# Windowed attention and two dense layers on one core: packed scores in 32-query strips, a third packed unit, new order keys and an early sine

## The chip, the cores and the metric

The kernel runs on one core of a Trainium2 chip. The metric is the device time of one execution in microseconds (us). Times come from repeated executions; the profile is of one execution.

## The reference, cut to what matters

Three steps follow one another: attention in which a query sees its own and the 63 keys before it, a dense layer with a squared ReLU, and a dense layer with h·cos(h). All arithmetic is on float32 values.

```python
# q, k, v: (4, 8, 576, 64)
scores = scale * np.matmul(q, k.transpose(0, 1, 3, 2))
rel = pos[:, None] - pos[None, :]
mask = (rel >= 0) & (rel < 64)
scores = np.where(mask, scores, -1e9)
scores = scores - np.max(scores, axis=-1, keepdims=True)
attn = np.exp(scores)
attn = attn / (np.sum(attn, axis=-1, keepdims=True) + 1e-09)
x = np.matmul(attn, v)            # then 2304 tokens x 512
h = np.maximum(x @ w_in, 0.0)     # w_in: 512 x 2048
x = h * h @ w_out                 # w_out: 2048 x 512
h = x @ w_in2
out = h * np.cos(h) @ w_out2
```

## The kernel before, in words

**Tokens and groups.** The 2304 tokens are cut into nine units of 256 tokens (n = 0 to 8). Attention runs by group (n, g): a unit and four of the eight heads (g = 0 or 1), 18 groups in all. Each group has two DMAs (its queries with keys, its values), a scores step on TensorE (PE), a softmax on VectorE (DVE) and ScalarE (ACT), one or two transpose steps and a product with v on PE, and then the result is split into a high and a low float32r part in X (or kept whole, for the last units).

**Two forms of a group.** Units 0 to 2 (`PACKED = 3`) take the unpacked form in `attention`: each window of 64 queries keeps its 128 scores, DVE adds a mask and takes the maximum in one instruction for each of eight blocks of 128 columns (L953), ACT takes eight exponentials of 128 columns (L959), and two transpose steps T of four transposes (L978) follow, one for each half of the heads. Units 3 to 8 take the packed form in `packed`: of each query's 128 columns only one of each pair (c, c + 64) can be inside the window, so DVE folds the second 64 columns over the first with a predicated copy (L736); everything after has 64 columns, and one transpose step (L777) does for the group. DVE spreads the transposed block again into two (L783), and the product with v is made of products of 64 by 64 by 64 (L795). Masks for the packed form are built on GpSimd ahead of the first packed group.

**The scores step** S (L723, L936) has 16 products for a group: 64 queries of one head (64 rows of the array, half e) are the stationary side, 128 keys the moving side. Two head halves e and two query halves c address the four 64-by-64 quarters of the array, which the source goes through in the innermost loops. The results of a head half stand in one PSUM bank.

**Dense layers.** Weights come as float32 words in 64-bit pairs, are put together on ACT and DVE, and split into a high and a low float32r part (`to_f32`, `convert_w`: L376, L330 on ACT, L388, L392, L414 on DVE). The first layer runs for each unit as products `ph` (L1785) and `accA` (L1111, L1178); the last four units run in a form with sums (L1624, L1702). The second layer's weights are converted beside it, stored to HBM (`convert_w2`) and loaded again. The second layer with the sine runs last (L1496, L1454), after about 452 us.

**Order.** Nothing is ordered by hand. Each step is an `op` with an estimated time on each engine that may take it, a key, what it depends on and what buffers it takes. `Plan.run` goes through time with these estimates; on each engine the earliest step starts next, and of steps that could start within 0.03 us of each other the one with the smallest key. The result is the fixed order in which each engine's queue gets its instructions; the SP queue, which issues the DMAs, is one of them. `START` and `MID` hold keys: of attention groups (`att`: key of the group and offset of its second part), of weight conversions (`conv`: key of the words, of the high and low part, of the load), of loads (`load`), and which steps a second engine may take (`cast`, `low`, `norm`, `upper`). `gap` lets a step on PE be preceded by filler matmuls (`keep_busy`, L318) where the plan sees PE idle ahead of it.

Of the kernel before, what the change touches and what calls it, by code (L numbers as in the profile page):

```python
# [9 lines left out]
F32 = mybir.dt.float32  # L10
# [6 lines left out]
P = 128  # L17
# [169 lines left out]
def dve_us(n, fast=False):  # L187
    return 0.065 + n / (1920.0 if fast else 960.0)
# [6 lines left out]
def pe_us(n, passes=1):  # L195
    return max(0.108, 0.0134 + passes * n / 2400.0)
# [2 lines left out]


PER1 = 22.7
PACKED = 3
MASK = I32
MARGIN = 0.7
MID = {'att': {3: (-3.1, 3.1),
         4: (38.0, 3.0),
         5: (32.8, 5.1),
         6: (13.5, 7.7),
         7: (22.0, 2.0),
         8: (19.0, 3.6)},  # L210
 'sum': (17, 19, 20, 25, 28, 39, 41, 42),
 'w2': (19, 20, 21, 40, 41, 42, 45, 48, 49, 50, 53, 55, 56, 57, 57, 58),
 'w2key': 65.5}

START = {'ahead': 4,
 'att': {(0, 0): (9.7, 7.0),
         (0, 1): (-98.1, 3.0),
         (1, 0): (-59.2, 6.9),
         (1, 1): (-139.0, 2.1),
         (2, 0): (21.1, 4.1),  # L220
         (2, 1): (14.9, 2.9)},
 'cast': (6, 7, 8, 9, 10, 11, 13),
 'conv': {0: (-53.4, -31.9, -41.6),
          1: (-44.5, 92.9, -84.7),
          2: (20.9, 7.3, 10.7),
          3: (-0.1, -29.5, 45.9),
          4: (11.3, 19.1, -71.8),
          5: (-74.1, 99.6, 33.1),
          6: (33.8, -82.0, 22.0),
          7: (23.9, 58.2, -23.9),  # L230
          8: (157.2, 44.2, -41.9)},
 'diag': (),
 'exact': 2,
 'halves': 4,
 'load': {(0, 0): (-163.6, -82.2),
          (0, 1): (-141.7, -117.8),
          (1, 0): (-12.1, 12.9),
          (1, 1): (0.9, -50.2),
          (2, 0): (-29.6, -13.5),
          (2, 1): (-46.2, 47.2)},  # L240
 'low': (4, 5, 6),
 'norm': ((0, 0, 1), (1, 0, 0), (1, 1, 0), (2, 0, 1), (2, 1, 0), (2, 1, 1)),
 'pool': (),
 'upper': ((0, 0), (0, 1), (1, 0))}


@with_exitstack
def kernel(
# [89 lines left out]
    def bank(buf, shape, name):  # L338
        return ps_q.tile([P, *shape], F32, tag=f"q{buf.slot}", name=name)
# [341 lines left out]
    def packed(n, g, key, sp, k_s=None):  # L681
# [8 lines left out]

        smb = R["sm"].buf()

        qb, vb, pbuf, ptb = (R[x].buf() for x in ("qk", "v", "pb", "PT"))

        def room(name, buf, at, shape):
            return ap_.tile([P, *shape], F32, tag=name, name=f"{name}_{nm}")

        sb = [R["q"].buf() for _ in range(2)]
        tb = R["q"].buf()
# [11 lines left out]
        l0 = dma(k_qk, load_qk, P * 2 * QK * 4, [], [qb], order=[loaded[0]])  # L711
        l1 = dma(k_v, load_v, P * NR * 4 * D * 4, [], [vb], order=[l0, loaded[1]])
        loaded[:] = l0, l1

        def scores(eng):
            t["pb"] = room("pb", pbuf, 0, [2, 2, HB, WINDOW])
            t["S"] = [bank(b, [2, HB, P], f"S_{nm}_{e}") for e, b in enumerate(sb)]
            for r in range(2):
# [10 lines left out]
        o_s = op({"PE": 0.35 + 8 * 0.104}, k_s, scores, [l0, turns["q"]], [*sb, pbuf], [qb])  # L729

        def gather(eng, e):
            if e == 0:
# [33 lines left out]

        def norm(eng):
            pb = t["pb"].rearrange("p e r i q -> p (e r i) q")
            nc.vector.tensor_tensor(
                pb, pb, t["sm"].rearrange("p e r i -> p (e r i)").unsqueeze(2)  # L770
                .to_broadcast([P, 4 * HB, WINDOW]), ALU.mult)

        def transp(eng):
            t["T"] = bank(tb, [2, 2, P], f"T_{nm}")
            for e in range(2):
# [10 lines left out]

        def weighted(eng):
            t["O"] = [bank(b, [2, P], f"O_{nm}_{i}") for i, b in enumerate(ob)]
            for r in range(2):
# [26 lines left out]
        o_t = op({"PE": 4 * pe_us(P) + 0.09}, late, transp, [o_n, o_setup], [tb], [pbuf])  # L816
        o_p = []
        for k in range(2):
            first = k == 0
            o_p.append(op({"DVE": dve_us(512)}, late, lambda q, k=k: spread(q, k), [o_t, o_pack[2], *o_p],  # L820
                          [ptb] if first else [], [tb] if first else [tb, ptb], lat=MARGIN))
        free = ([s1_held[0]] if n >= len(x_col) else [g1_last[m] for m in x_before[n]]) if g else []
        o_v = op({"PE": 0.35 + 16 * 0.053}, late, weighted, [l1, *o_p, *free], [*ob], [ptb, vb])
        turns["q"] = o_v

        cs = slice(2 * g, 2 * g + 2)
# [1252 lines left out]
```

## Time and profile before

| | us |
|---|---|
| median of the timed runs | 839.39 (838.63 to 839.53, 3 runs) |
| the profiled execution | 837.72 |
| its span, first to last instruction | 836.0 |
| PE busy in the span | 828.8 (99%) |
| DVE, ACT, GpSimd busy | 651.0 (78%), 477.0 (57%), 15.6 (2%) |

The span is the time from the first to the last instruction; the execution's own time has 1.7 us around it. A matmul's record reaches from its start to a modelled end, and records overlap, so what a block of matmuls costs is read from its start to the start of the next block. PE's clock was granted in full (1.00) in every stretch shown below.

### The profile page before, as it was taken

To read this page: it belongs to the slowest core of one execution; us is meant where nothing else is said; L and a number is where in the kernel's file an instruction comes from. 1 tells how busy PE (TensorE), PEld (TensorE's weight loads), DVE (VectorE), ACT (ScalarE), POOL (GpSimd) and SP (SyncE) were. 2 spreads that over 40 slices of the span, in tenths; PEclk is the share of its full clock that TensorE was granted. 3 is DMA by queue.
4 is the path that set the end of the run, shared out by engine and by line. 5 is a ranking of instruction groups with operands and counts; after the bars stand their busy time and mean duration, and the time that the engine had idled before them with its cause. 6 is when DMAs were issued, how large, how long until landed. Compare 5 with 4: busy or idle time off the path is not lost.

```text
span 836.0 us, 14646 instructions
## 1 busy us (share of the span) xinstructions
PE 828.8 (99%) x5572; PEld 724.5 (87%) x5572; DVE 651.0 (78%) x1338; ACT 477.0 (57%) x1048; POOL 15.6 (2%) x42
## 2 busy tenths in 40 slices
PE   8999999999999999999999999999999999999998
PEld 8898889998778888888888999988999988999986
DVE  6999769888877887676868788885788885788851
ACT  7998676564565835344412656663656563656642
POOL 2100020000000000000000000000000000000000
PEclk9999999999999999999999999999999999999999
DMA  9884096947978559998898593052643062642011
GB/s 348 320 334 139 3 323 235 347 173 243 362 269 289 209 197 356 328 336 310 308 333 359 226 422 145 1 227 113 252 153 112 1 237 102 252 167 99 1 38 38
DMA packets 39798, 181.96 MB, mean 218 GB/s; under 512 B 4016, under 2 KB 6576, under 8 KB 27440
## 3 DMA queue, kind: packets, MB, share of 16 engines
q1 hardware_dynamic: 39728, 181.03, 58.8%
q8 instruction: 44, 0.72, 0.3%
q14 instruction: 26, 0.21, 0.1%
HBM read 129.63 MB, written 51.38 MB: 217 GB/s over the span
## 4 chain that ended last, share of the span: by engine, by line
PE 90%; DVE 5%; ACT 2%; DMA 1%; issue 1%; SPq 0%; ACTq 0%; DVEq 0%
PE accB L1454 24%; PE x L1496 12%; PE ph L1785 11%; PE accC L1702 10%; PE accA L1111 10%; PE z L1496 6%; PE x L1624 4%; PE y L1496 3%; PE z L1624 2%; PE O L795 1%; PE S L723 1%; PE accA L1178 1%; PE y L1624 1%; DMA qk<-in_qk_dram 1%; DMA w2b_dram<-w2b 1%; PE T L777 1%
## 5 line engine op out<-in xcount | busy, mean ns | idle before, releaser
L1785 PE MATMUL ph<-X,W_in_w_dram 128*128 128x512 f32 (+1 forms) x624 | 124.2, 344 | 0.0
L1111 PE MATMUL accA<-g,W_in_w_dram 128*128 128x512 f32 (+1 forms) x528 | 111.8, 355 | 0.0
L1785 PEld LDWEIGHTS ph<-X,W_in_w_dram 128*128 128x128 f32 x624 | 98.5, 189 | 14.2 <-issue 0.5
L1454 PE MATMUL accB<-wo,gb_e 128*128 128x512 f32 x432 | 100.1, 389 | 0.0
L1111 PEld LDWEIGHTS accA<-g,W_in_w_dram 128*128 128x128 f32 x528 | 86.3, 189 | 14.6 <-issue 2.1
L1454 PEld LDWEIGHTS accB<-wo,gb_e 128*128 128x128 f32 x432 | 81.0, 188 | 16.5
L1454 PE MATMUL accB<-wo,gb_b 128*128 128x512 f32 x216 | 54.3, 393 | 0.0
L1454 PE MATMUL accB<-wo,gb_a 128*128 128x512 f32 x216 | 54.2, 393 | 0.0
L376 ACT ACTIVATE raw_in_w_dram<-raw_in_w_dram 128x1024 f32<-128x1024 f32 x32 | 36.6, 1148 | 19.6 <-DMA raw_in_w_dram<-in_w_dram 19.6
L1454 PEld LDWEIGHTS accB<-wo,gb_b 128*128 128x128 f32 x216 | 40.2, 188 | 7.5
L1454 PEld LDWEIGHTS accB<-wo,gb_a 128*128 128x128 f32 x216 | 40.2, 188 | 7.2
L1512 ACT ACTIVATE held<-x 128x384 f32<-128x384 f32 x72 | 34.4, 481 | 20.1 <-PE x L1496 20.1
L1496 PE MATMUL x<-X,wb 128*128 128x384 f32 x216 | 45.7, 337 | 0.0
L1496 PE MATMUL x<-X,wa 128*128 128x384 f32 x216 | 45.3, 335 | 0.0
L1702 PE MATMUL accC<-g_k,W_in_w_dram 128*128 128x512 f32 x192 | 44.3, 389 | 0.0
L1702 PEld LDWEIGHTS accC<-g_k,W_in_w_dram 128*128 128x128 f32 x192 | 36.0, 188 | 7.3
L1428 DVE TENSOR_TENSOR gb_e<-keep,gb_e 128x384 fp32r<-128x384 f32 x48 | 25.9, 554 | 20.9 <-ACT gb_e L330 20.6
L1496 PEld LDWEIGHTS x<-X,wa 128*128 128x128 f32 x216 | 38.7, 188 | 2.4
L1075 ACT ACTIVATE r<-ph 128x512 f32<-128x512 f32 (+1 forms) x52 | 26.1, 502 | 23.9 <-PE ph L1785 22.9
L1496 PEld LDWEIGHTS x<-X,wb 128*128 128x128 f32 x216 | 38.5, 188 | 0.3
L330 ACT ACTIVATE gb_e<-keep 128x384 fp32r<-128x384 f32 x48 | 24.2, 517 | 25.4 <-PE accB L1454 25.4
L1088 DVE TENSOR_TENSOR g<-r,g 128x512 fp32r<-128x512 f32 (+1 forms) x52 | 30.2, 581 | 6.2 <-ACT r L1083 5.4
(222 smaller groups left out, 1697.4 us busy)
## 6 DMA issues: line engine op xcount, KB each, us to landing
raw_in_w_dram<-in_w_dram SPq DMA_DIRECT2D x32, 1024.0 KB, 8.3
wa<-w2a_dram SPq DMA_DIRECT2D x24, 1024.0 KB, 7.2
wb<-w2b_dram SPq DMA_DIRECT2D x24, 768.0 KB, 7.6
qk<-in_qk_dram SPq DMA_DIRECT2D x17, 576.0 KB, 6.0
v<-in_v_dram SPq DMA_DIRECT2D x18, 512.0 KB, 4.7
w1s_dram<-s SPq DMA_DIRECT2D x8, 1024.0 KB, 6.2
w2a_dram<-w2a SPq DMA_DIRECT2D x8, 1024.0 KB, 5.2
w2o_dram<-w2o SPq DMA_DIRECT2D x8, 1024.0 KB, 5.1
```

Of the source, the lines that this page charges most:

```text
L330: nc.scalar.activation(o, i, AF.Copy, scale=scale)
L376: nc.scalar.activation(hw, hw, AF.Prelu, scale=2.0**-112, alpha=-(2.0**32))
L1075: nc.scalar.activation(t["r"], ph()[:, 0:w], AF.Relu)
L1088: nc.vector.tensor_tensor(t["g"][:, 1], t["r"], f32(t["g"][:, 0]), ALU.subtract)
L1111: nc.tensor.matmul(self.acc[i][:, k, :], w[:, j % 2, wl, m * P:m * P + P], t["g"][:, gl, :], start=(j == 0 and p == 0 and k == 0 and self. ...
L1428: nc.vector.tensor_tensor(t["g"][:, 1], r(), f32(t["g"][:, 0]), ALU.subtract)
L1454: nc.tensor.matmul(acc[0], t["g"][:, gl, m * P:m * P + P], wb.tile[:, k % 2, wl], start=(k == 0 and i == 0), stop=(k == NJ - 1 and i == 2))
L1496: nc.tensor.matmul(ps[x], wb.tile[:, i, wl, c * P:c * P + P], piece(o, c, xl), start=(first and c == 0 and k == 0), stop=(last and c == 1 ...
L1512: return b, op({"ACT": act_us(H)}, key - 6, lambda e: nc.scalar.activation(r_at(b), ps[x], AF.Copy), [dep, o_rooms], [b], [buf], lat=0.39)
L1624: nc.tensor.matmul(ps[x], wb.tile[:, i, wl, c * P:c * P + P] if src is pb or i > 1 else wb.tile[:, wl, i, c * P:c * P + P], piece1(o, c, x ...
L1702: nc.tensor.matmul(acc[0][:, 0], wb.tile[:, k % 2, wl, m * P:m * P + P], t["g"][:, gl, :], start=(k == 0 and p == 0), stop=(k == NJ - 1 an ...
L1785: nc.tensor.matmul(t["ph"][:, 0:u.w], wb.tile[:, j % 2, wl, c * P:c * P + P], u.x(xl, c), start=(c == 0 and k == 0), stop=(c == NCC - 1 an ...
```

## The change

- In `packed`, the scores of a group are 32 products instead of 16: strips of 32 queries (`NEAR`), the first of each 64 with all 128 keys, the second without the first 32 keys (96 keys, written from column 32 on). A strip addresses a part of the array of 64 rows and 32 columns. The estimate for the step (`SCORES`) has the same value as before, 1.182.
- `PACKED` goes from 3 to 2: unit 2 takes the packed form. `packed` gets the lines of `attention` that let early units have fillers, other rooms for tiles (`guest`, for units 0 and 1, which do not come here) and a normalization on GpSimd where `norm` says so. The margin of 0.7 us that the plan adds after the normalization and the spreading holds for n > 2 only.
- `START` and `MID` get other values throughout: keys of attention, loads and conversions, the places at which the sums and the second layer's conversions are let in, and which steps a second engine may take. `ahead` goes from 4 to 3.
- One sine of a single column is put on ACT after the last conversion of the second layer's weights, and the second layer's activations come after it.

```diff
-PACKED = 3
+PACKED = 2
+NEAR = 32
+SCORES = 1.182
 MID = {'att': ...
- 'w2': (19, 20, 21, 40, 41, 42, 45, 48, 49, 50, 53, 55, 56, 57, 57, 58),
- 'w2key': 65.5}
+ 'w2': (21, 28, 33, 43, 45, 47, 47, 48, 48, 48, 49, 49, 49, 49, 49, 50),
+ 'w2key': 91.0}
...
-START = {'ahead': 4,
- 'att': {(0, 0): (9.7, 7.0),
-         (0, 1): (-98.1, 3.0),
-         (1, 0): (-59.2, 6.9),
-         (1, 1): (-139.0, 2.1),
-         (2, 0): (21.1, 4.1),
-         (2, 1): (14.9, 2.9)},
- 'cast': (6, 7, 8, 9, 10, 11, 13),
- 'conv': {0: (-53.4, -31.9, -41.6),
-          1: (-44.5, 92.9, -84.7),
+START = {'ahead': 3,
+ 'att': {(0, 0): (8.9, 1.4),
+         (0, 1): (-175.7, 7.7),
+         (1, 0): (-57.0, 9.5),
+         (1, 1): (-254.5, 5.3),
+         (2, 0): (21.4, 2.5),
+         (2, 1): (-4.3, 11.3)},
+ 'cast': (9, 11, 12, 14, 15),
+ 'conv': {0: (-55.8, -57.4, -66.7),
+          1: (-164.1, 139.2, -121.7),
...
- 'low': (4, 5, 6),
- 'norm': ((0, 0, 1), (1, 0, 0), (1, 1, 0), (2, 0, 1), (2, 1, 0), (2, 1, 1)),
+ 'low': (4, 6),
+ 'norm': ((0, 0, 1), (1, 0, 0), (1, 1, 0), (2, 0, 0), (2, 0, 1)),
...
- 'upper': ((0, 0), (0, 1), (1, 0))}
+ 'upper': ((0, 0), (0, 1))}
...
-                        for c in range(2):
-                            q0 = (2 * i + c) * WINDOW
+                        for c in range(4):
+                            q0 = i * P + c * NEAR
+                            lo = c % 2 * NEAR
                             nc.tensor.matmul(
-                                t["S"][e][HALF[c], r, i], t["qk"][HALF[e], r, q0:q0 + WINDOW],
-                                t["qk"][HALF[e], r, UA + q0:UA + q0 + P],
+                                t["S"][e][c * NEAR:c * NEAR + NEAR, r, i, lo:],
+                                t["qk"][HALF[e], r, q0:q0 + NEAR],
+                                t["qk"][HALF[e], r, UA + q0:UA + q0 + P - lo],
                                 start=(r == 0 and i == 0), stop=(r == 1 and i == HB - 1),
...
-        o_n = op({"DVE": dve_us(512) + 0.02}, late, norm, [o_r], use=[smb, pbuf], lat=MARGIN)
+        o_n = op({"POOL": pool_us(512, True)} if (n, g, 0) in START["norm"] else {"DVE": dve_us(512) + 0.02}, late, norm, [o_r], use=[smb, pbuf], lat=MARGIN if n > 2 else None)
...
+    def sine_table(e):
+        nc.scalar.activation(cp.tile([P, 1], F32, name="turned"), hpi, AF.Sin)
+
+    o_sine = op({"ACT": 1.5}, base1, sine_table, [w2_taken[0]], lat=0.0)
+    begun[0] = o_sine
```

## Rows read from the trace of the kernel before

**Rows 1.** The page's first part: busy time, share of the span, instructions.
```profile
PE 828.8 (99%) x5572; PEld 724.5 (87%) x5572; DVE 651.0 (78%) x1338; ACT 477.0 (57%) x1048; POOL 15.6 (2%) x42
```

**Rows 2.** Busy time by stage: length, engines with instructions, clock, DMA share, GB/s.
```profile
24.00:42.00 18.00, 17.60 (x230) 16.04 (x230) 16.73 (x41) 17.07 (x41) 1.33 (x1) 1.00 0.83 307
...
100.00:300.00 200.00, 199.78 (x2193) 170.15 (x2192) 165.11 (x350) 123.49 (x375) 5.88 (x13) 1.00 0.73 261
300.00:452.00 152.00, 151.82 (x670) 125.33 (x670) 112.29 (x188) 60.00 (x90) 0.00 (x0) 1.00 0.90 327
```

**Rows 3.** Timeline of PE in the start: start, length, line, operation, tiles, shape, count.
```profile
18.81 4.29 PE L318 MATMUL T<-still 128*128 128x128 f32 x36
...
24.18 2.08 PE L1785 MATMUL ph<-X,W_in_w_dram 128*128 128x256 f32 x15
```

**Rows 4.** Timeline of DVE in the start, steps for the first weight tile.
```profile
18.16 0.68 DVE L334 CAST X<-O 128x512 fp32r<-128x512 f32 x1
...
20.33 1.22 DVE L392 CUSTOM_DVE_ANT_0 raw_in_w_dram<-raw_in_w_dram,cw_in_w_dram 128x2048 uint16<-128x2048 uint16 x1
...
23.18 1.21 DVE L414 TENSOR_TENSOR W_in_w_dram<-raw_in_w_dram,W_in_w_dram 128x1024 fp32r<-128x1024 f32 x1
```

**Rows 5.** Timeline of ACT in the start, the cast of the same tile.
```profile
21.59 1.16 ACT L330 ACTIVATE W_in_w_dram<-raw_in_w_dram 128x1024 fp32r<-128x1024 f32 x1
```

**Rows 6.** Timeline of PE, blocks of unit 2 and the first packed S.
```profile
100.21 0.60 PE L978 MATMUL T<-ident,pb 128*128 128x128 f32 x4
100.56 1.64 PE L1785 MATMUL ph<-X,W_in_w_dram 128*128 128x512 f32 x6
...
114.29 1.15 PE L993 MATMUL O<-PT,v 128*64 128x64 f32 x32
115.37 1.10 PE L723 MATMUL S<-qk 64*64 64x128 f32 x32
116.41 2.34 PE L1785 MATMUL ph<-X,W_in_w_dram 128*128 128x512 f32 x9
```

**Rows 7.** Timeline of PE, packed blocks: an S by itself, and S behind O.
```profile
141.98 1.10 PE L723 MATMUL S<-qk 64*64 64x128 f32 x32
143.01 0.98 PE L1111 MATMUL accA<-g,W_in_w_dram 128*128 128x256 f32 x6
...
202.84 1.16 PE L795 MATMUL O<-PT,v 64*64 64x64 f32 x64
203.83 1.05 PE L723 MATMUL S<-qk 64*64 64x128 f32 x32
204.81 1.67 PE L1111 MATMUL accA<-g,W_in_w_dram 128*128 128x512 f32 x6
```

**Rows 8.** Timeline of PE in windows 162.85:162.89 and 163.40:163.44, records of one S.
```profile
162.59 0.56 PE L723 MATMUL S<-qk 64*64 64x128 f32 x12
...
163.18 0.51 PE L723 MATMUL S<-qk 64*64 64x128 f32 x12
```

**Rows 9.** Waits of PE, 24.2 to 304 us: total, times, longest.
```profile
PE T L978 <- ACT g L1079: 0.4, 1, 0.4
PE T L777 <- DVE pb L769: 0.2, 1, 0.2
```

**Rows 10.** Timeline of ACT: last conversion of the second matrix, and the sine's table.
```profile
427.29 1.13 ACT L376 ACTIVATE raw_in_w_dram<-raw_in_w_dram 128x1024 f32<-128x1024 f32 x1 [11.26 <-DMA raw_in_w_dram<-in_w_dram]
...
458.82 1.28 ACT L1403 ACT_TABLE_LOAD   x1 [0.94 <-DVE rr_a L1399]
```

**Rows 11.** Timeline of PE at the start of the last stage.
```profile
458.23 1.55 PE L1702 MATMUL accC<-g_k,W_in_w_dram 128*128 128x512 f32 x6
...
469.69 2.24 PE L1454 MATMUL accB<-wo,gb_a 128*128 128x512 f32 x9
```

**Rows 12.** Exponentials by line: count, ns min/median/max, first and last start.
```profile
L959 ACT ACTIVATE pb<-pb,mm x48: 384/387/408, 6.5 to 107.7; 128x128 f32<-128x128 f32 x48
...
L758 ACT ACTIVATE pb<-S,mm x96: 296/320/353, 119.3 to 278.2; 128x64 f32<-128x64 f32 x96
```

More of the change, by code (lines that the diff above doesn't have):

```diff
@@ L201 @@
 PER1 = 22.7
-PACKED = 3
+PACKED = 2
 MASK = I32
 MARGIN = 0.7
[L205 to L211, printed above, removed]
- 'w2': (19, 20, 21, 40, 41, 42, 45, 48, 49, 50, 53, 55, 56, 57, 57, 58),
- 'w2key': 65.5}
-START = {'ahead': 4,
- 'att': {(0, 0): (9.7, 7.0),
-         (0, 1): (-98.1, 3.0),
-         (1, 0): (-59.2, 6.9),
-         (1, 1): (-139.0, 2.1),
-         (2, 0): (21.1, 4.1),
-         (2, 1): (14.9, 2.9)},
- 'cast': (6, 7, 8, 9, 10, 11, 13),
- 'conv': {0: (-53.4, -31.9, -41.6),
-          1: (-44.5, 92.9, -84.7),
[L225 to L231, printed above, removed]
+NEAR = 32
+SCORES = 1.182
+MID = {'att': {3: (16.9, 2.0), 4: (29.6, 0), 5: (36.2, 0.3), 6: (-2.7, 2.0), 7: (1.1, 3.0), 8: (9.9, 8)},
+ 'sum': (13, 20, 22, 27, 37, 38, 43, 44),
+ 'w2': (21, 28, 33, 43, 45, 47, 47, 48, 48, 48, 49, 49, 49, 49, 49, 50),
[10 more added lines that the diff above has]
+          1: (-164.1, 139.2, -121.7),
+          2: (72.7, -65.0, 8.6),
+          3: (0.5, -34.8, 116.1),
+          4: (8.4, 52.8, -154.9),
+          5: (-126.3, 121.3, 77.1),
+          6: (189.0, 66.3, -45.6),
+          7: (10.1, 106.2, -49.2),
+          8: (71.3, -10.9, 65.3)},
  'diag': (),
@@ L234 @@
  'halves': 4,
[L235 to L240, printed above, removed]
- 'low': (4, 5, 6),
- 'norm': ((0, 0, 1), (1, 0, 0), (1, 1, 0), (2, 0, 1), (2, 1, 0), (2, 1, 1)),
+ 'load': {(0, 0): (-165.0, -118.5),
+          (0, 1): (-133.5, -152.3),
+          (1, 0): (-36.9, 8.8),
+          (1, 1): (7.7, -22.3),
+          (2, 0): (-41.0, 21.2),
+          (2, 1): (-82.5, 8.4)},
+ 'low': (4, 6),
+ 'norm': ((0, 0, 1), (1, 0, 0), (1, 1, 0), (2, 0, 0), (2, 0, 1)),
  'pool': (),
- 'upper': ((0, 0), (0, 1), (1, 0))}
+ 'upper': ((0, 0), (0, 1))}
 @with_exitstack
@@ L691, in packed @@
         smb = R["sm"].buf()
-        qb, vb, pbuf, ptb = (R[x].buf() for x in ("qk", "v", "pb", "PT"))
-        def room(name, buf, at, shape):
-            return ap_.tile([P, *shape], F32, tag=name, name=f"{name}_{nm}")
+        guest = n < 2 and g == 1
+        if guest:
+            qb, vb, ptb = (R["W"].buf() for _ in range(3))
+            pbuf = ptb
+        else:
+            qb, vb, pbuf, ptb = (R[x].buf() for x in ("qk", "v", "pb", "PT"))
+        def room(name, buf, at, shape):
+            if not guest:
+                return ap_.tile([P, *shape], F32, tag=name, name=f"{name}_{nm}")
+            if at == 0:
+                t[buf] = wp.tile([P, 4 * DM], F32, tag=f"W{buf.slot}", name=f"{name}_{nm}")
+            size = math.prod(shape)
+            flat = t[buf][:, at:at + size]
+            dims = " ".join("abcd"[:len(shape)])
+            return flat.rearrange(
+                f"p ({dims}) -> p {dims}", **dict(zip("abcd", shape)))
         sb = [R["q"].buf() for _ in range(2)]
@@ L710, in packed @@
         k_qk, k_v = START["load"].get((n, g), (k_s - 3, key - 2))
-        l0 = dma(k_qk, load_qk, P * 2 * QK * 4, [], [qb], order=[loaded[0]])
-        l1 = dma(k_v, load_v, P * NR * 4 * D * 4, [], [vb], order=[l0, loaded[1]])
-        loaded[:] = l0, l1
+        l0 = dma(k_qk, load_qk, P * 2 * QK * 4, [], [qb], order=[None if guest else loaded[0]])
+        l1 = dma(k_v, load_v, P * NR * 4 * D * 4, [], [vb], order=[l0, None if guest else loaded[1]])
+        if not guest:
+            loaded[:] = l0, l1
         def scores(eng):
@@ L720, in scores @@
                     for e in range(2):
[L721 to L722 removed]
+                        for c in range(4):
+                            q0 = i * P + c * NEAR
+                            lo = c % 2 * NEAR
                             nc.tensor.matmul(
[L724 to L725 removed]
+                                t["S"][e][c * NEAR:c * NEAR + NEAR, r, i, lo:],
+                                t["qk"][HALF[e], r, q0:q0 + NEAR],
+                                t["qk"][HALF[e], r, UA + q0:UA + q0 + P - lo],
                                 start=(r == 0 and i == 0), stop=(r == 1 and i == HB - 1),
                                 skip_group_check=True)
[L729 removed]
+        o_s = op({"PE": SCORES}, k_s, scores, [l0, turns["q"]], [*sb, pbuf], [qb],
+                 gap=40 if n < 2 else 0)
         def gather(eng, e):
@@ L774, in transp @@
             t["T"] = bank(tb, [2, 2, P], f"T_{nm}")
+            keep_busy(t["T"][:, 0, 0])
             for e in range(2):
@@ L814, in packed @@
         o_r = op({"DVE": 0.42}, late, recip, ex, use=[smb])
-        o_n = op({"DVE": dve_us(512) + 0.02}, late, norm, [o_r], use=[smb, pbuf], lat=MARGIN)
-        o_t = op({"PE": 4 * pe_us(P) + 0.09}, late, transp, [o_n, o_setup], [tb], [pbuf])
+        o_n = op({"POOL": pool_us(512, True)} if (n, g, 0) in START["norm"] else {"DVE": dve_us(512) + 0.02}, late, norm, [o_r], use=[smb, pbuf], lat=MARGIN if n > 2 else None)
+        o_t = op({"PE": 4 * pe_us(P) + 0.09}, late, transp, [o_n, o_setup], [tb], [pbuf],
+                 gap=40 if n < 3 else 0)
         o_p = []
         for k in range(2):
-            first = k == 0
+            first = k == 0 and not guest
             o_p.append(op({"DVE": dve_us(512)}, late, lambda q, k=k: spread(q, k), [o_t, o_pack[2], *o_p],
-                          [ptb] if first else [], [tb] if first else [tb, ptb], lat=MARGIN))
+                          [ptb] if first else [], [tb] if first else [tb, ptb], lat=MARGIN if n > 2 else None))
         free = ([s1_held[0]] if n >= len(x_col) else [g1_last[m] for m in x_before[n]]) if g else []
-        o_v = op({"PE": 0.35 + 16 * 0.053}, late, weighted, [l1, *o_p, *free], [*ob], [ptb, vb])
+        o_v = op({"PE": 0.35 + 16 * 0.053}, late, weighted, [l1, *o_p, *free], [*ob], [ptb, vb],
+                 gap=40 if n < 3 else 0)
         turns["q"] = o_v
```

4 lines of the change are left out of this document (3 added, 1 removed).

## The prediction

> **What bounds the kernel now.** I read the page's first part, then the busy time by stage, and then the start, the attention blocks and the hand-over to the last stage in order of time. TensorE (PE) is busy for 828.8 of the 836.0 us [rows 1]. By stage it is busy almost without a break from 24 us on: 17.60 of 18 us, 199.78 of 200 us between 100 and 300 us, 151.82 of 152 us after that [rows 2]. A busy PE row can hide slack, because overlapping matmuls count as one busy stretch, so I take every price below from the distance between starts and not from durations. Two things follow. First, from 24 us on a microsecond comes back only if PE is given less to do, or if one of its few real waits goes: the waits listed for 24 to 304 us are two, 0.4 and 0.2 us [rows 9]. Second, ahead of 24 us PE is not doing wanted work all the time: before the first product of the first layer, at 24.18 us, it runs a row of 36 filler matmuls from 18.81 us [rows 3]. What it waits for there is the first weight tile. On VectorE (DVE) the addition that puts this tile's words together (L392) starts at 20.33 us, on ScalarE (ACT) the cast of its high part runs from 21.59 to 22.75, and the subtraction for the low part (L414) from 23.18 to 24.39 [rows 4, 5]. So the span is 24 us of start, some 800 us of a PE that is full, and the end. The last stage (after 452 us) and the end keep their instructions, so the change can act in the start, on the attention's PE blocks, and by new waits.
>
> **Part 1, unit 2 packed.** An unpacked group has on PE the scores (S), two blocks of four transposes (T) and the product with v (O); a packed one has S, one T block and O. One T block moves the next start by 100.56 - 100.21 = 0.35 us [rows 6]. O is 115.37 - 114.29 = 1.08 us in the unpacked form [rows 6] and 203.83 - 202.84 = 0.99 us in a packed one followed by S [rows 7]; the difference belongs to the neighbour that comes next (part 2), so I count O as equal. Two groups lose one T block each: 2 x 0.35 = -0.7 us of PE. The rest of the group is on ACT and DVE: eight exponentials of 128 columns at 387 ns become eight of 64 at 320 ns [rows 12], and so on. PE was full there, with both other engines beside it, so this is worth nothing by itself; if it helps the start, it is in part 3. The masks for the packed form are now built on GpSimd earlier, where that engine is nearly idle (1.33 us in 24 to 42 us [rows 2]): nothing.
>
> **Part 2, strips of 32 queries.** Sixteen products per group with 64 queries and 128 keys become 32 with 32 queries and 128 or 96 keys by turns. In the trace of before, each product shows as two records. The 32 records of one S run in fours: the first three fours are over at 162.59 + 0.56 = 163.15 us, the last three at 163.18 + 0.51 = 163.69 us [rows 8]. From the third four to the eighth it is thus 0.54 us, or 0.11 us for a round of four records side by side in the four quarters of the array. Eight rounds are 0.88 us, and with the entry a block costs 143.01 - 141.98 = 1.03 us [rows 7]. With strips there are eight places for 64 records, again eight rounds. The strips with 96 keys have places of their own and finish early; those with 128 keys still need 8 x 0.11 us in theirs. So I expect no gain: 0 for each of the 14 packed groups. No row shows eight places at work, so I bound it. If the time went with the columns, 7/8 of 0.88 us is left: -0.11 x 14 = -1.5 us. If only four places work at a time, 16 rounds of a mean (0.11 + 0.083)/2 us are 1.54 us: +0.66 x 14 = +9.2 us. I take 0, because the quarters do run side by side in rows 8, and nothing in these rows shows a limit at four.
>
> The Trainium skill, "TensorE: Matmul & The Clock Gate", section "Wait — 56ns, not 53.3ns?", speaks against strips: small matmuls would never start less than about 25 ns apart. By that rule 64 records would take at least 1.6 us, and the sum would be about 8 us higher. The trace disagrees so far: the 64 records of a packed O take 0.99 us [rows 7], 15 ns each.
>
> A second thing is sure to change. S right after a packed O, which divides the array as the old S did, makes the pair cost 204.81 - 202.84 = 1.97 us [rows 7]. Where the two divide it differently (unpacked O, then packed S), the pair costs 116.41 - 114.29 = 2.12 us [rows 6]. There are four pairs of the first kind (at 127.45, 202.84, 215.40 and 229.12 us), and with strips none can be. That is 4 x 0.15 = +0.6 us if all four stay neighbours; the new order may part some, or make more. I take +0.3, with ends at 0 and +0.6.
>
> **Part 3, new keys (START, MID).** The list of first-layer products does not change: with "ahead" at 3 or 4 and "halves" at 4, half 0 runs through its four steps and half 1 follows. What changes is the priority of attention and weight conversion on ACT, DVE, GpSimd and the SP queue. At the very start the order of loads by key is the same up to the first weight tiles. For the first weight tile the words' key goes from -53.4 to -55.8 and that of its high and low part from -31.9 to -57.4, against -59.2 and -57.0 for the first half of group (1,0) and -52.3 and -47.5 for its second. So the words still stand behind the first half of (1,0), but the high and low part now go ahead of everything of that group. In the trace the low part starts 0.43 us after the high part's end (22.75 to 23.18 [rows 4, 5]), most of which the new key can take away: -0.3 us. Ends: -1.9 us if the addition also starts at once after the cast at 18.16 us, which ends 1.5 us ahead of it [rows 4], and +1.2 us if one more conversion step (1.16 us [rows 5]) comes in front. Between 24 and 42 us DVE and ACT are busy nearly throughout (16.73 and 17.07 of 18 us [rows 2]), so a gain at 24 us holds only if they keep up; that is why I stay near the small end.
> For the waits after that, two are in the trace, 0.6 us in all [rows 9]. The new order can remove them or make others; I take 0, with ends -0.6 and +2 (five more waits like the 0.4). The conversions of the second matrix are spread anew, the last of them no longer held until the second unit's products are well on. Their last one landed late in before: ACT idled 11.26 us for that transfer, at 427.29 us [rows 10], 25 us ahead of the stage that needs it (452 us). So some microseconds either way are covered; past that they would hold the whole of PE.
>
> **Part 4, the early sine.** The sine's table is loaded at 458.82 us for 1.28 us [rows 10]. PE works on other products at 458.23 [rows 11], and the first product that needs this sine starts at 469.69 us [rows 11], so nothing waits for it: 0. Moved ahead, the load and one small activation sit behind the last conversion on an ACT that is 60 of 152 us busy in 300 to 452 us [rows 2]: also 0. Without that cover it would cost 1.28 us once.
>
> **Sum.** -0.7 (T blocks) + 0.3 (pairs) + 0 (strips) - 0.3 (first weight tile) + 0 (waits) + 0 (sine) = -0.7 us: a span of 835.3 instead of 836.0 us. The profiled execution took 837.72 us, 1.67 us under the median of the three timed runs, 839.39; the same difference put on the median gives 838.7 us. What a measurement of this kernel can tell from no change is about 0.2%, 1.7 us; 837.7 to 841.1 us therefore counts as the same.
>
> **The rivals.**
> 1. The start shrinks (faster). The addition for the first weight tile goes ahead of (1,0), the two waits go: -0.7 - 1.9 - 0.6 = -3.2 us, 836.2 us. For it: 36 fillers in the row before 24.18 us. Against it: DVE and ACT are the narrow place there and the keys of the addition barely move against (1,0).
> 2. Strips pay by their columns (faster): -0.7 + 0.3 - 0.3 - 1.5 = -2.2 us, 837.2 us. Against it: a 128-key strip has its own place and its own eight rounds.
> 3. Eight strips do not run at a time (slower): the front of PE feeds four places and no more, in each of 14 packed S blocks. 9.2 - 0.7 + 0.3 - 0.3 = +8.5 us, 847.9 us; it decides over the sum as soon as an S block costs over 0.18 us more than now. For it: no row shows eight. The 25 ns rule of the Trainium skill, above, would end near here.
> 4. New waits in the attention's stage (slower): DVE, 165.11 of 200 us busy between 100 and 300 us [rows 2], is behind with a group's normalization, and PE, which takes its steps in order, stands before T. At 0.4 us [rows 9] in 6 to 14 of the groups that is +2.4 to +5.6 us, with the -0.7 a time of 841 to 844 us. It decides from six such waits on. Against it: the old order has hardly any.
>
> **How the numbers follow.** Chances: forecast (all terms near the taken values, within 0.2%) 0.42; start 0.26; strips by columns 0.10; strips four at a time 0.10; new waits 0.12. Faster is 0.26 + 0.10 = 0.36, the same 0.42, slower 0.10 + 0.12 = 0.22. The likeliest is 838.7 us; its own range is 837.7 to 841.1. For 8 in 10, the low end goes to 836.0, which takes in most of the start's gain, and the high end to 843.0, which takes in most of the new waits and leaves the slow strips out.
>
> **What would show it.** Right: S blocks in the new trace with 64 records and 1.0 to 1.1 us from start to next start; one T block for each group of unit 2; the first product at 23.5 to 24.3 us; no new idle time of PE after 42 us; the table load some time before 452 us with no change on PE. Wrong: S blocks of 0.9 (rival 2) or over 1.2 us (rival 3); a first product before 23 us (rival 1); a list of waits before T with more than a microsecond in it (rival 4), or a PE that stands still near 450 us for the last conversion.

## The result and the profile after

The changed kernel takes 843.53 us (median of 6 runs, 842.52 to 844.06), the kernel before in the same comparison 839.01 us. The ratio is 1.0054, with a 95% interval of 1.0042 to 1.0066: 4.5 us slower, above the upper end of the forecast range (843.0). The profiled execution took 844.06 us with a span of 842.3; where the two traces are set side by side, the distance is therefore 6 us and not 4.5.

First the lines of the page of after that answer to [rows 1], and the stages of [rows 2] (length, then busy time and instructions of PE, PEld, DVE, ACT, POOL, then the clock, the DMA share and GB/s).

```profile
PE 832.8 (99%) x6076; PEld 723.4 (86%) x6076; DVE 656.9 (78%) x1325; ACT 471.5 (56%) x1044; POOL 14.3 (2%) x40
```

```profile
24.00:42.00 18.00, 17.60 (x262) 15.98 (x261) 17.04 (x42) 17.59 (x44) 6.17 (x12) 1.00 0.85 320
100.00:300.00 200.00, 198.54 (x2653) 167.94 (x2653) 161.10 (x331) 112.72 (x364) 0.00 (x0) 1.00 0.68 242
300.00:452.00 152.00, 151.98 (x662) 123.97 (x662) 113.75 (x185) 63.86 (x97) 0.00 (x0) 1.00 0.88 327
```

PE is as full as before, at the same clock, and does the same products. Between 300 and 452 us it starts 662 instructions where it started 670 [rows 2]. That is a stage in which the change edits no product. Its products themselves have become slower. To see it, take the timeline of PE in this stage (start, length, line, operation, tiles, shape, count), once of the kernel before and once of the changed one.

```profile
342.49 1.52 PE L1624 MATMUL x<-X,w1b 128*128 128x512 f32 x6
343.85 1.52 PE L1624 MATMUL x<-X,w1a 128*128 128x512 f32 x6
345.21 1.52 PE L1624 MATMUL y<-X,w1a 128*128 128x512 f32 x6
```

```profile
346.38 1.56 PE L1643 MATMUL x<-X,w1b 128*128 128x512 f32 x6
347.78 1.56 PE L1643 MATMUL x<-X,w1a 128*128 128x512 f32 x6
349.18 1.56 PE L1643 MATMUL y<-X,w1a 128*128 128x512 f32 x6
```

Six products take 343.85 - 342.49 = 1.36 us before, 227 ns from start to start, and 347.78 - 346.38 = 1.40 us after, 233 ns. No wait stands between them in either. The difference is 6 ns a product. The dense layers have 3840 products of several kinds, and not all kinds slow down.

The attention's blocks of after, as [rows 6, 7] show those of before: an S by itself, and two S behind O. The last one holds a pause of PE that is new. It is the only new entry in the list of waits between 24.2 and 304 us (compare [rows 9]), which names it, with "issue" as its releaser: PE waited for nothing that the profile shows.

```profile
145.86 1.14 PE L736 MATMUL S<-qk 64*32 64x128 f32 x64
146.93 0.62 PE L1130 MATMUL accA<-g,W_in_w_dram 128*128 128x256 f32 x3
...
102.72 1.16 PE L812 MATMUL O<-PT,v 64*64 64x64 f32 x64
103.82 1.14 PE L736 MATMUL S<-qk 64*32 64x128 f32 x64
104.89 1.42 PE L1130 MATMUL accA<-g,W_in_w_dram 128*128 128x512 f32 x5
...
258.62 1.16 PE L812 MATMUL O<-PT,v 64*64 64x64 f32 x64
259.71 1.07 PE L736 MATMUL S<-qk 64*32 64x128 f32 x54
262.24 0.42 PE L736 MATMUL S<-qk 64*32 64x96 f32 x10 [1.46 <-issue]
262.59 1.65 PE L1130 MATMUL accA<-g,W_in_w_dram 128*128 128x512 f32 x6
```

```profile
PE S L736 <- issue: 1.5, 1, 1.5
PE T L997 <- ACT g L1098: 0.4, 1, 0.4
```

An S by itself costs 146.93 - 145.86 = 1.07 us, where it cost 1.03 [rows 7]. A pair O, S costs 104.89 - 102.72 = 2.17 us, where it cost 1.97 [rows 7].

The start and the table of the sine, as in [rows 3 to 5, 10]:

```profile
20.65 1.22 DVE L389 CUSTOM_DVE_ANT_0 raw_in_w_dram<-raw_in_w_dram,cw_in_w_dram 128x2048 uint16<-128x2048 uint16 x1
...
23.50 1.22 DVE L411 TENSOR_TENSOR W_in_w_dram<-raw_in_w_dram,W_in_w_dram 128x1024 fp32r<-128x1024 f32 x1
...
24.50 1.72 PE L1804 MATMUL ph<-X,W_in_w_dram 128*128 128x256 f32 x12
...
439.54 1.28 ACT L1935 ACT_TABLE_LOAD   x1
```

All of PE's distances from start to start, summed by kind and set against before, say where the 5.9 us went by which PE's last product ends later in the profiled execution (worked out from all starts of the two traces, the stages cut at the same products in both; their times are those of before; us):

```
                 start   24-147   147-285   285-462   462-end    all
first product    +0.32                                          +0.32
T blocks                 -0.71    -0.08                         -0.79
O blocks                 +0.13    +0.42                         +0.55
S blocks                 +0.22    +2.56 (1.81 the pause)        +2.78
products                 +0.71    -0.16     +1.92     +0.54     +3.01
```

The block of 259.71 us takes 262.59 - 259.71 = 2.88 us to the next start, 1.81 more than an S of 1.07, of which PE stands idle for 1.46.

Half of the 5.9 us is in the dense layers' products, which the prediction did not touch at all. About 2.5 us of that is slower pace. The 0.54 us after 462 us stand at one place, the hand-over to the last stage, where PE now waits for the step on ACT that writes `held`; first before, then after:

```profile
461.70 1.20 PE L1496 MATMUL y<-X,wa 128*128 128x384 f32 x6
463.79 1.20 PE L1496 MATMUL z<-X,wb 128*128 128x384 f32 x6
```

```profile
466.99 1.20 PE L1515 MATMUL y<-X,wa 128*128 128x384 f32 x6
468.45 1.32 PE L1515 MATMUL x<-X,wb 128*128 128x384 f32 x6 [0.26 <-ACT held L1531]
469.61 1.21 PE L1515 MATMUL z<-X,wb 128*128 128x384 f32 x6
```

The two blocks take 469.61 - 466.99 = 2.62 us, where they took 2.09. All eight traces with the new order and the early sine lose 0.4 to 0.5 us here, and none of the eight with the old order does. Which of the two makes it was not tried.

### The profile page after: what moved, and what is told of

It is laid out like the page before. It is cut to its first block, busy times and chain, and to the rows that moved or that the text cites. A ratio compares the mean times of both kernels' runs of the same rounds, so it can differ in the third digit from the quotient of the medians.

```text
span 842.3 us, 15643 instructions
## 1 busy us (share of the span) xinstructions
PE 832.8 (99%) x6076; PEld 723.4 (86%) x6076; DVE 656.9 (78%) x1325; ACT 471.5 (56%) x1044; POOL 14.3 (2%) x40
## 4 chain that ended last, share of the span: by engine, by line
PE 93%; DVE 3%; ACT 2%; DMA 1%; issue 1%; SPq 0%; ACTq 0%
PE accB L1473 24%; PE ph L1804 13%; PE accA L1130 12%; PE x L1515 11%; PE accC L1721 8%; PE z L1515 6%; PE x L1643 5%; PE y L1515 3%; PE z L1643 3%; PE S L736 2%; PE O L812 2%; PE y L1643 1%; PE accA L1197 1%; DMA qk<-in_qk_dram 1%; PE T L793 1%
## 5 line engine op out<-in xcount | busy, mean ns | idle before, releaser
L1804 PE MATMUL ph<-X,W_in_w_dram 128*128 128x512 f32 (+1 forms) x624 | 125.9, 346 | 0.0
L327 ACT ACTIVATE gb_e<-keep 128x384 fp32r<-128x384 f32 x48 | 24.3, 518 | 26.7 <-PE accB L1473 26.6
L773 ACT ACTIVATE pb<-S,mm 128x64 f32<-128x64 f32 x112 | 33.3, 326 | 7.8 <-DVE mm L770 7.8
```

The lines of the kernel that those rows point to most:

```text
L327: nc.scalar.activation(o, i, AF.Copy, scale=scale)
L773: nc.scalar.activation(t["pb"][:, e, r, i], t["S"][e][:, r, i, 0:WINDOW], AF.Exp, bias=t["mm"][:, e, r, i:i + 1], scale=SCALE, accum_out=t ...
L1804: nc.tensor.matmul(t["ph"][:, 0:u.w], wb.tile[:, j % 2, wl, c * P:c * P + P], u.x(xl, c), start=(c == 0 and k == 0), stop=(c == NCC - 1 an ...
```

## The experiments

**The theory, called A.** The changed kernel allocates one more tile: the early sine's result, `cp.tile([P, 1], F32, name="turned")`, which takes 32 bytes of each partition. It lies ahead of the ring of weight tiles, so that the ring and the pools behind it move by 32 bytes, while X and the pools on the other side stay. The products' moving and stationary operands thereby stand differently to each other. By their addresses in the compiled program, X and the weights agreed modulo 256 bytes before (both leave the remainder 192); after, the weights are at 224. Theory A: the spacing of the products goes by this distance, and about 3 us of the loss are due to it. Its rivals: the strips themselves, the new order, and waits by the packed unit 2. Each run is compared with runs of the kernel before on the same chip, and in the expectations a time that stands alone is against those (838.1 to 838.7 us). Differences in us are between medians. The ratio is worked out from all runs, so the two can differ by up to 0.8 us.

**The 32 bytes alone.** The kernel before, plus an unused tile:

```diff
+    shift = cp.tile([P, 8], F32, name="shift")
+    nc.vector.memset(shift, 0.0)
```

> The kernel before with one tile of 32 bytes (and a memset of it) put behind the constants, so that weights, g and the rest stand 32 bytes further on against X, as in the changed kernel; nothing else. Theory A (addresses): +3 us, 839.0 becomes about 842.0, with 512-column products against X at 233 ns. Theory B: no change, 839.0.

Measured: 841.07 us against 838.14, ratio 1.0033 (1.0021 to 1.0045), +2.9 us. Its timeline has the same products at the spacing of after:

```profile
344.60 1.56 PE L1626 MATMUL x<-X,w1b 128*128 128x512 f32 x6
346.00 1.56 PE L1626 MATMUL x<-X,w1a 128*128 128x512 f32 x6
347.40 1.56 PE L1626 MATMUL y<-X,w1a 128*128 128x512 f32 x6
```

1.40 us for six. A tile that nobody reads makes the kernel 2.9 us slower; no sine, strip or new order is in it. (The instruction that fills it is not the cause: a larger tile with the same instruction, below, costs 0.35 us.)

**A larger tile in the changed kernel.** If the distance decides, a tile that restores it should bring the time back.

```diff
-        nc.scalar.activation(cp.tile([P, 1], F32, name="turned"), hpi, AF.Sin)
+        nc.scalar.activation(cp.tile([P, 16], F32, name="turned")[:, 0:1], hpi, AF.Sin)
```

> The changed kernel with one edit: the tile that the early sine writes gets 64 bytes per partition instead of 4, so that all tiles behind it stand as in the kernel before modulo 64 bytes (weights and g at the same remainder as X; in the changed kernel they are 32 bytes off X). Theory A (addresses): in the trace of the changed kernel, products of 512 columns whose stationary and moving operands differ by 32 modulo 64 bytes take 233 ns from start to start, those at the same remainder 228; 384 columns 173.4 against 174.9 in the kernel before. About 1000 x 5 ns less 1000 x 1.5 ns less 0.4 us is 3 us: 843.5 becomes about 840.5. Theory B (the slower time comes from strips and order alone): no change, 843.5. In both the order is the same instruction for instruction, so the pause inside a scores block near 260 us stays if it belongs to the code's loading.

Measured: 844.0 us, 1.0070 (1.0058 to 1.0082). The theory's period of 64 bytes was wrong. In the traces read up to then a period of 128 bytes was possible, so the tile was made twice as wide (`[P, 32]`):

> The changed kernel with the early sine's tile made 128 bytes wide instead of 4, nothing else. Theory A, in the form that the run with 64 bytes left it (the spacing of matmuls goes by the remainder of the two operands' addresses modulo 128 bytes): every remainder is again what it was before, so the 2.9 us of the shift are gone: about 840.6, with the strips, the new order and the packed unit 2 still in it (+1.5 to +2 against before). If remainders have nothing to do with it and the time lies in the new order and the strips: 843.5 to 844, as the changed kernel.

Measured: 845.87 us, 1.0088 (1.0075 to 1.0101): worse than with 32 bytes, and again against the expectation. Either the addresses are not the cause in this kernel, or the period is longer still. Two runs settled that, the kernel before with an unused tile of 128 bytes and one of 256 bytes, otherwise as the shift by 32 (`[P, 32]` and `[P, 64]`):

> The kernel before with an unused tile of 128 bytes per partition ahead of the weight ring, nothing else. The run with the sine's tile at 128 bytes had its 512-column products at 232.9 ns where the operands stood 128 bytes apart modulo 256 and at 228.9 where they did not. If that is the address (theory A with a period of 256 bytes or more): +0.6 before 147 us, +1.6 between 284 and 459, +3.7 after, +5.8 in all. If it was the changed order of that kernel and 128 bytes are harmless: +0.

> The kernel before with an unused tile of 256 bytes per partition ahead of the weight ring. If the spacing goes by the distance of the operands modulo 256 bytes: as before, within 0.3. If every departure from the old distance costs, or the period is longer (512 bytes or more): +1 or more.

Measured: with 128 bytes 843.78 us, 1.0070 (1.0056 to 1.0085), +5.1; with 256 bytes 838.93 us, 1.0010 (0.9998 to 1.0021), +0.35 and not told from zero. The same instructions, moved by 128 bytes, lose 5.1 us, and moved by 256 nothing. The last stage shows it in the timelines of the kernel before and of the shift by 128:

```profile
609.99 1.20 PE L1496 MATMUL y<-X,wa 128*128 128x384 f32 x6
611.03 1.20 PE L1496 MATMUL x<-X,wb 128*128 128x384 f32 x6
```

```profile
612.98 1.22 PE L1498 MATMUL y<-X,wa 128*128 128x384 f32 x6
614.04 1.22 PE L1498 MATMUL x<-X,wb 128*128 128x384 f32 x6
```

1.04 us for six products of 384 columns before (611.03 - 609.99), 1.06 with the shift.

**The changed kernel with nothing moved.** The early sine is written into a spare column of the tile that holds pi/2, so no room is taken.

```diff
-    hpi = cp.tile([P, 1], F32, name="hpi")
+    half_pi = cp.tile([P, 2], F32, name="half_pi")
+    hpi = half_pi[:, 0:1]
...
-        nc.scalar.activation(cp.tile([P, 1], F32, name="turned"), hpi, AF.Sin)
+        nc.scalar.activation(half_pi[:, 1:2], hpi, AF.Sin)
```

> The changed kernel with the early sine written into the second column of the tile that already holds pi/2, so that it takes no room and no other tile moves; strips, new order and packed unit 2 as in the changed kernel. Theory A (what the tile's room costs is the moved operands): the products' spacings return to those of before, 3.0 us by the sums of the products' rows (0.7 before 147 us, 1.9 between 284 and 459, 0.5 after), so +1.4 to +2 against before. Rival (the sine itself, or the order, holds the products up, whatever the addresses): +4.5 as the changed kernel.

Measured: 840.47 us against 838.68, 1.0030 (1.0016 to 1.0044), +1.8 instead of +4.5. The same products stand at 1.36 us for six again:

```profile
344.17 1.52 PE L1644 MATMUL x<-X,w1b 128*128 128x512 f32 x6
345.53 1.52 PE L1644 MATMUL x<-X,w1a 128*128 128x512 f32 x6
```

Together with the shift by 32 this settles the first 2.7 to 2.9 us: the room of the sine's tile, and not the sine.

**The strips.** First alone, in the order of before: only the loop of the scores is changed, for its 12 packed groups.

```diff
-                        for c in range(2):
-                            q0 = (2 * i + c) * WINDOW
+                        for c in range(4):
+                            q0 = i * P + c * NEAR
+                            lo = c % 2 * NEAR
```

> The kernel before with the scores of its 12 packed groups in strips of 32 queries; same keys, same order, no sine, addresses as before. By the blocks in the changed kernel's trace an S by itself goes from 1.124 to 1.165 us of PE and a pair O then S from 2.06 to 2.25: 8 x 0.04 + 4 x 0.19 = 1.1 us, 840.1. If the doubled count of instructions also makes PE wait for its code inside a block, up to 1.8 us more for each pair so hit: 841 to 843. If strips do nothing, 839.0.

Measured: 840.11 us, 1.0022 (1.0009 to 1.0035), +2.0, with a wide spread (838.37 to 843.7 in 12 runs). Then the other way round, the changed kernel with the old scores, with each of the three rooms for the sine:

> The changed kernel with the old scores of 64 queries; the order, the sine and its 4-byte tile stay. Strips' theory: 9 S by themselves and 5 pairs give back 9 x 0.04 + 5 x 0.19 = 1.3 us, and the pause of 1.8 us at 260 us with two smaller ones (0.4 us) go: 843.5 becomes 840 to 842. Theory A alone: 843.5.

> The changed kernel with the tile of 128 bytes and with the old scores, two products of 64 queries in place of four of 32. What is left of the change is the packed unit 2, the new numbers of the plan and the early sine. Theory A: the run without strips was 4.4 above before, of which 2.9 is the shift, so about +1.5 here: 839.5. If the strips cost what they cost alone in the old order (+2), this kernel is 1 to 2 us below the one with the tile of 128 bytes and strips; if they cost nothing, the two agree.

> The changed kernel with the sine written beside pi/2 (no tile) and with the old scores of 64 queries: only the packed unit 2, the new numbers of the plan and the early sine are left. If the strips make the +1.8 that the kernel without the tile still had: 838.7, as before, or 0.5 less (two T blocks saved, -0.7, one more pair O, S, +0.2). If the new order makes it: +1 to +1.8 with the strips gone.

Measured: with the tile as changed 842.58 us, 1.0048 (1.0035 to 1.0060); with 128 bytes 844.2 us, 1.0062 (1.0050 to 1.0074); with no tile 838.56 us, 1.0003 (0.9990 to 1.0017). In the last one nothing has moved. Without tile and strips, packed unit 2, new order and early sine together change nothing that can be measured; the strips are the rest, 1.8 us between medians. The two kernels that this compares ran on different chips, and their intervals just meet (1.0016 to 1.0044 and 0.9990 to 1.0017). With 128 bytes the strips cost 1.7 us on one chip, with intervals that do not meet (1.0075 to 1.0101 and 1.0050 to 1.0074). With 32 bytes the result does not fit so well: with the strips 1.0054 (1.0042 to 1.0066), without them 1.0048, a difference of 0.5 us and less than the intervals. This kernel without strips should stand 2.9 above before if the parts add up, and it stands 4.4 above (2.9 to 5.0 by the interval).

Where the strips lose it is in the trace. Without them (and without the tile) the pair that holds the pause of after stands like this, and with them (still without the tile) like that:

```profile
257.79 1.16 PE L811 MATMUL O<-PT,v 64*64 64x64 f32 x64
258.77 1.06 PE L736 MATMUL S<-qk 64*64 64x128 f32 x32
259.76 1.45 PE L1129 MATMUL accA<-g,W_in_w_dram 128*128 128x512 f32 x5
```

```profile
258.01 1.16 PE L813 MATMUL O<-PT,v 64*64 64x64 f32 x64
259.11 1.07 PE L737 MATMUL S<-qk 64*32 64x128 f32 x54
260.98 0.42 PE L737 MATMUL S<-qk 64*32 64x96 f32 x10 [0.80 <-issue]
261.33 3.03 PE L1131 MATMUL accA<-g,W_in_w_dram 128*128 128x512 f32 x12
```

259.76 - 257.79 = 1.97 us against 3.32. Five S blocks of the new order stand behind an O, at 0.20 us each (2.17 - 1.97); nine stand alone, at 0.04 (1.07 - 1.03); the pause adds 3.32 - 2.17 = 1.15 here, from start to start. 5 x 0.20 + 9 x 0.04 + 1.15 = 2.5 us in this execution, for 1.8 in the medians.

In the new order the pause always comes after the 54th record of this block, in after (1.46 us idle), in this kernel (0.80) and in those with a tile of 64 (0.30) and 128 bytes (0.32): a fixed place in the program and a changing length. The strips only in the old order have such a pause too, at another block:

```profile
233.28 0.65 PE L725 MATMUL S<-qk 64*32 64x128 f32 x26
235.21 0.85 PE L725 MATMUL S<-qk 64*32 64x96 f32 x38 [1.28 <-issue]
```

What fits is that PE's own instructions come late. The page of after has more of them to fetch than that of before (44 packets, 0.72 MB); the strips add 448 matmul records, and an O with a strip S behind it starts 128 records in 2.2 us.

```profile
q8 instruction: 48, 0.79, 0.4%
```

The five traces with strips have 47 or 48 packets in this queue and one such pause each; the eleven without strips have 44 and none. In each of the five, a packet of 16 KB of this queue starts within the pair that holds the pause, and PE goes on 1.3 to 1.6 us after it has landed. But packets also start within pairs that have no pause (at 247.23 us in after). It was not tried by an experiment of its own and stays a likely reading.

**Unit 2 packed alone.** The kernel before with unit 2 packed (`PACKED = 2` and the code for it), with the old order, the old scores and no early sine.

> The kernel before with unit 2 packed as in the changed kernel, but with the old scores, the old numbers of the plan and no early sine. The first theory, of the prediction: two T blocks fewer at 0.36 us each, 837.4, if no wait comes in their place. The rival: the old numbers put some packed step of unit 2 ahead of what it needs, and a wait of up to 1.5 us on TensorE takes the gain: 838.1 to 839.

Measured: 842.15 us, 1.0048 (1.0036 to 1.0060), +3.5. The list of PE's waits from 24.2 to 304 us has what the old order lacks:

```profile
PE ph L1807 <- DVE X L876: 2.0, 3, 1.1
PE O L815 <- ACT r L1105: 1.0, 1, 1.0
PE T L796 <- ACT r L1105: 0.9, 1, 0.9
PE T L796 <- DVE pb L787: 0.6, 2, 0.4
PE T L1000 <- DVE pb L991: 0.5, 1, 0.5
PE T L796 <- POOL pb L787: 0.5, 1, 0.5
```

5.5 us in these six lines, in an execution of 844.21 us. So the packed unit and the new numbers belong together: in the old order the packed unit costs 3.5 us, and with the new one the two change nothing. The new order without the packed unit was not tried.

**Can the distance be used?** In the shift by 32 bytes, the 384-column products of the last stage had become faster while others became slower. Over all 1008 of them, from all starts of the two traces, the mean is 173.7 ns against 174.5; the expectations below take 173.4 and 174.9, and so a gain of 1.5 us where 0.8 is there. So the pieces that these products read were moved, in the kernel before:

```diff
-        return X[:, half].rearrange("p l c n -> p (l c n)")[:, k * H:k * H + H]
+        return X[:, half].rearrange("p l c n -> p (l c n)")[:, k * H + 8:k * H + H + 8]
```

(the pieces in `x_more` likewise). By 8 elements, 32 bytes, at first:

> The kernel before with the pieces of phase 3's moving operand laid 32 bytes further on, so that the 1008 products of 384 columns have operands with different remainders modulo 128 bytes; all else as before. Theory A, from the spacings read in the two traces (384 columns: 174.9 ns where the remainders agree, 173.4 where they are 32 apart): 1008 x 1.5 ns = 1.5 us less, about 836.6. If the remainder matters only by chance of these two traces, no difference: 838.1.

Measured: 838.64 us against 838.69, 0.9999 (0.9988 to 1.0010): nothing. This run moved more than the 32 bytes. `x_more` got 128 bytes more room, and by the compiled addresses it began 128 bytes earlier. Its 288 products of 384 columns thus had their pieces 96 bytes below the weights modulo 256 instead of 32 above, and the 48 products of 512 columns that read it went from 227 to 232 ns. With 224 bytes it got 256 bytes more, which leaves the remainders as meant. The other side, 56 elements or 224 bytes, which puts the weights 32 bytes above the pieces modulo 256, as in after:

> The kernel before with the moving pieces of phase 3 laid 224 bytes further on. The run with 32 bytes the other way had its 384-column products at 174.1 ns instead of 173.4 (before: 174.9) and no gain in the time. If the side counts (the changed kernel had the stationary operand 32 bytes above the moving one modulo 256), 1008 x 1.5 ns = 1.5 us less than before. If not: as before within 0.3.

Measured: 835.52 us against 838.68, 0.9965 (0.9952 to 0.9977), -3.2 us, twice the expectation, and for the larger part in another place than expected, as the sums below show. The same with the new order and the packed unit 2:

> The changed kernel without the sine's tile (its result goes beside pi/2), with the old scores of 64 queries, and with the moving pieces of phase 3 laid 224 bytes further on, so that the 384-column products stand as in the changed kernel (173.4 ns) while all the others stand as before. Theory A: the run with the tile of 128 bytes and no strips was 5.5 above before, 5.8 to 6.2 of it in the products' spacing, so -0.5 without it, and 1008 x 1.5 ns = 1.5 less by the pieces: -2 against before. Rival: +1.5 (what the run without strips left beside its shift), with no gain from the pieces.

Measured: 836.01 us, 0.9969 (0.9956 to 0.9981), -2.7. Both are faster than the kernel before and the changed one, and beyond the pieces the change gives the second nothing over the first. In the timelines of the last stage, before and then with the pieces moved by 224 bytes:

```profile
605.80 2.24 PE L1454 MATMUL accB<-wo,gb_a 128*128 128x512 f32 x9
607.88 0.69 PE L1496 MATMUL x<-x_more,wb 128*128 128x384 f32 x3
```

```profile
605.17 2.20 PE L1454 MATMUL accB<-wo,gb_a 128*128 128x512 f32 x9
607.22 0.69 PE L1496 MATMUL x<-x_more,wb 128*128 128x384 f32 x3
```

The nine products of accB take 2.08 us before and 2.05 here, though neither of their operands was moved. Mean distances from start to start within a block, worked out from all starts of each trace (ns; weights of `wa`, `wb` and `wo` in the last stage, `w1b` ahead of it):

```
weights moved by:         0 (before)   32     128    256     0, pieces by 224
x<-X,w1b      512 columns   226.8     233.3  233.2  226.6       226.8
accB<-wo,gb_a 512 columns   230.6     226.9  229.7  230.6       226.9
accB<-wo,gb_e 512 columns   227.0     230.7  231.9  227.0       226.7
x<-X,wb       384 columns   175.4     173.4  175.7  175.4       173.4
y<-X,wa       384 columns   173.3     173.3  175.7  173.3       173.3
```

Three columns here are plain: what is moved by 256 is as before, 128 slows most kinds and the time most, 32 slows some and speeds others. The last column shows that a product's own two operands are not the whole of it: accB with gb_a is 3.7 ns faster with the neighbours' operands moved. In the kernel before, too, the operands of all these products have the same remainder of 192 by the compiled addresses, and yet accB has two paces. PE's distances after 462 us sum to 2.8 us less with the pieces moved: 1.9 of it in the 864 products of accB and 0.9 in the 1008 of 384 columns. The expectation had only the latter; the rest of the gain was luck.

## Why the prediction was wrong, step by step

- **The early sine, costed at 0: the step that failed.** The prediction followed its instructions, the table load and the activation, and found them covered. That holds: the load is at 439.54 us, 1.28 us long, and nothing on PE waits for it. What was left out is that the step allocates a tile. Its 32 bytes alone cost 2.9 us. The prediction said that "the change can act in the start, on the attention's PE blocks, and by new waits"; the room acts on products that the change does not edit, which is none of the three. No term, bound or rival had this, and the stretch that loses most by it, 285 to 462 us with +1.92 us, is one for which the prediction weighed only conversions and the sine.
- **Strips, costed at 0 for the block: nearly right.** 64 records take 1.07 us from start to start, inside the 1.0 to 1.1 that was named as the sign; eight places do work side by side, 1.07 us / 64 = 17 ns a record. The mechanism was right, and the block was mis-sized by 0.04 us. Rival 3 is out. The rule of the Trainium skill beside it ("TensorE: Matmul & The Clock Gate", "Wait — 56ns, not 53.3ns?", no less than about 25 ns from start to start) is not what this trace shows.
- **Pairs O, S, costed at +0.3: the direction right, both factors too small.** The prediction took 4 pairs at 0.15 and halved the sum. The new order has 5, and each costs 0.20 more: +1.0. The price was taken from an unpacked O before a packed S [rows 6], the nearest row, and it was not the same thing.
- **The pause in an S block: no term.** 0.3 to 1.5 us of idle PE, 0.7 to 1.8 from start to start, at one place. The prediction bounded the waits by semaphores; "issue" is not one.
- **Unit 2 packed, costed at -0.7: right for the T blocks.** T blocks between 24 and 147 us sum to 3.24 instead of 3.95 us. What the packed unit saves, the new order's pairs and an S of 1.35 us at 203 us (in the kernel without strips too) give back in part.
- **First weight tile, costed at -0.3: wrong, and small.** The subtraction starts at 23.50 instead of 23.18 us, and the first product at 24.50, outside the 23.5 to 24.3 named. In the other traces of the new order it starts at 24.3 to 24.8, with one exception at 23.6. In those of the old order it starts at 23.7 to 25.6, so the traces do not tell the two orders apart here.
- **Waits, costed at 0: nearly right.** PE's list up to 304 us has 0.4 us beside the pause, for 0.6 before [rows 9]. The wait for `held` at 468 us, 0.3 us idle and 0.5 from start to start, is new and had no term. Rival 4 was not what happened; the kernel with the packed unit in the old order shows that it would have been, without the new numbers.

Put together from the runs: 2.9 (the tile's room) + 1.8 (strips with pairs and pause) + 0.0 (unit 2, order, sine) = 4.7 us, for 4.5 measured. The prediction had 0, +0.3 and -1.0 for the three. The room alone would have left the time inside the range (838.7 + 2.9 = 841.6); with the strips it is outside. That the parts add up is good to about 1.5 us, as the kernel with the tile as changed and the old scores shows.

What stays open: how the distance between tiles slows a product, why neighbours count, and whether the pause is the fetch of instructions. An unused tile moves the tiles of all engines behind it, so the runs do not tell whether PE's own reads get in each other's way or those of other engines and DMAs get in PE's.

## What to carry to other kernels

Read an edit for what it allocates as well as for what it issues: on an engine that is full, a tile of 32 bytes that moves thousands of products' operands can cost more than all the work that the edit saves. When a change slows code that it does not touch, compare start-to-start distances of the same product in both traces, and run the old kernel with an unused tile of the same size. A product shape that runs at two speeds within one trace can be a sign that placement has something to give; here it was.

## What the runs showed of the hardware that was not expected

- Moving the weights against X changes the pace of products that wait for nothing: 227 to 233 ns for 512 columns, 173 to 176 ns for 384. A shift by 128 bytes costs 5.1 us and one by 256 bytes 0.35, not told from zero; a period of 256 bytes is what this placement shows. A product's own distance does not settle its pace, since its neighbours' operands count too.
- Products of the kernel before already had two paces for one shape: accB with gb_a 230.6 ns, with gb_e 227.0. Moving neither operand, but those of the products between, brought both to about 227; the kernel is 3.2 us faster, with 1.9 us less in accB by the traces.
- PE can stand still in the middle of a block with no semaphore to wait for, 1.46 us in after, in a stretch that otherwise starts 128 records of small matmuls within some 2.2 us.
